# The beginning of a Fourier transform with two feed-forward layers: x on two queues, one contiguous load, w_out's conversion moved, banks copied out earlier

## The chip, the cores and the metric

The kernel runs on one core of a Trainium2 chip. The metric is the time of one execution on the device in microseconds, as the median of three runs. Five engines work side by side, each through its own list of instructions in order: PE multiplies matrices (PEld is its loading of weights), DVE, ACT and POOL work on elements, and SP does nothing but start transfers between memories (DMAs). ACT and POOL can start DMAs too. They wait for each other by semaphores. Products of PE land in banks of the accumulation memory (PSUM), from which DVE or ACT has to copy them before a bank can be used anew.

## The reference

```python
X = np.fft.fft(x, axis=1)                 # x: (2, 3008, 256)
X = np.fft.fft(X, axis=2).real            # -> (6016, 256)
h = X @ w_in                              # w_in (256, 2048)
g = np.where(h > 0.0, h, np.exp(np.minimum(h, 0.0)) - 1.0)     # ELU
X = g @ w_out                             # w_out (2048, 256)
h = X @ w2_in
g = np.maximum(h, 0.0) + alpha * np.minimum(h, 0.0)            # PReLU
out = g @ w2_out
```

The weights are given as float64.

## The kernel before, in words

The transform along the sequence is split in two (3008 = 47 x 64). Stage A (`stage_a`, L143) multiplies x by a 96 x 96 matrix `f47`; x of a batch comes in four pieces c0 to c3 of 96 partitions (`load_x`, L132). The result `uc` is stored to memory as `ud` (`store_u`, L152) and loaded again with other axes on the partitions as `vt` (`load_v`, L164), 1 MB for each block. Stage B (`stage_b`, L195 and L196) multiplies `vt` by `r64` and leaves `zt`, a block of up to 512 columns split in a rounded high part and the rest, `hi` and `lo`. `delta` (L172) makes a correction row from `vt` that goes through memory (`nd`) and comes back as `zb` (`load_zb`, L183). The transform along the 256 columns is folded into the first weights (`w_fold`, L257). There are 2 batches of 3 blocks, and each block's columns come in two halves t = 0 and 1, the frequencies and their mirror images.

Float64 weights are read as pairs of integers and made into float32 on the chip (`conv_y` on ACT, L229; `conv_s`, three operations on DVE, L239 to L243), half a chunk at a time; `w_split` (L282 on ACT, L283 on POOL) makes the hi and lo parts of a chunk of w_out or of the second layer's weights.

Then come 192 ticks, 96 for each layer. A tick t is one block and one slice of 128 of the 2048 hidden columns: `gemm1` (L305) into two PSUM tiles, on DVE `pt` and two `ht` (L386 to L388) in layer 1, the exponential of the ELU on ACT (L403, L404), a tick later the combine on DVE (L419, in layer 2 L421), another tick later `hi` (L395, ACT) and `lo` (L413; POOL in layer 1, DVE in layer 2), and with a lag of three ticks `gemm2` (L319), which adds up in four banks `acc`, one for each output half d and column half t. `SEGS` lists 16 segments of 8 or 16 ticks; at a segment's end, one tick after its last `gemm2`, `evac` copies the four banks out (L350 on DVE for t = 0, L348 on ACT for t = 1). The next segment's first `gemm2` needs them free. The order of everything else is written by hand: `START` lists what happens ahead of tick 0, and tables such as `CONV1`, `CONV2`, `STAGE_A1` and `LOAD_V` hang the rest on ticks, in one of three places of a tick (`pre`, `mid`, `end`). In the function `tick` the order in the program is

```python
        if t - LAG - 1 >= 0 and ticks[t - LAG - 1][2] == ticks[t - LAG - 1][4]:
            evac(*ticks[t - LAG - 1])
        ...
        for fn in end:
            fn()
        if t - LAG in st:
            s = st.pop(t - LAG)
            gemm2(*ticks[t - LAG], s["hi"], s["lo"])
```

Of the kernel before, what the change touches and what calls it, by code (L numbers as in the profile page):

```python
# [7 lines left out]
F32 = mybir.dt.float32  # L8
# [64 lines left out]
def tile_fft_moe_elu_moe_prelu(  # L73
# [296 lines left out]

    def tick(t, pre, mid, end):
# [17 lines left out]
        if t - 2 in st:  # L389
            s = st[t - 2]  # L390
            n = s["n"]
            hi = wk.tile([128, 2, 512], F32R, tag="hi", name="hi")
            lo = wk.tile([128, 2, 512], F32R, tag="lo", name="lo")
            for i in parts(t - 2):
                act(out=hi[:, i, 0:n], in_=s["e"][:, i], func=ACTF.Copy)  # L395
            s["hi"], s["lo"] = hi, lo
# [12 lines left out]
        if t - 2 in st:  # L409
            s = st[t - 2]  # L410
            n = s["n"]
            for i in range(2):
                (nc.gpsimd if s["L"] == 1 else nc.vector).tensor_tensor(out=s["lo"][:, i, 0:n], in0=s["e"][:, i, :],  # L413
                                               in1=s["hi"][:, i, 0:n].bitcast(F32), op=ALU.subtract)
        if t - 1 in st:
            s = st[t - 1]
            if s["L"] == 1:
                for i in parts(t - 1):
                    stt(out=s["e"][:, i], in0=s["e"][:, i], scalar=-1.0, in1=s["h"][:, i], op0=ALU.add, op1=ALU.max)  # L419
            else:  # L420
                stt(out=s["e"], in0=s["e"], scalar=nal_sb[:, s["f"]:s["f"] + 1], in1=s["h"], op0=ALU.mult, op1=ALU.add)  # L421
# [26 lines left out]
    with tc.manual_schedule():  # L448
        nc.sync.dma_start(out=f47_sb, in_=f47)
        for c in range(4):  # L450
            load_x(0, c, 1 if c else 4)
# [150 lines left out]
```

## Time and profile before

| | |
|---|---|
| time before, median of 3 runs | 1028.83 us (1027.87 to 1028.89) |
| profiled execution: its own time / span of its instructions | 1030.7 / 1028.9 us |
| granted clock of PE, mean | 0.985 |
| PE busy | 995.4 us, 97% |
| DVE, ACT, POOL busy | 713.7, 681.8, 353.3 us |

The span is the time from the first to the last instruction; what lies outside it is start and end of the execution. A granted clock of 1.00 is 2.4 GHz, 0.50 is 1.2. The beginning is all that comes ahead of tick 0, the first 45 us. Tick 19 is near 150 us, tick 99 near 511, where layer 2 has just begun.

### The profile page before, as it was taken

To read this page: it belongs to the slowest core of one execution; us is meant where nothing else is said; L and a number is where in the kernel's file an instruction comes from. 1 tells how busy PE (TensorE), PEld (TensorE's weight loads), DVE (VectorE), ACT (ScalarE), POOL (GpSimd) and SP (SyncE) were. 2 spreads that over 40 slices of the span, in tenths; PEclk is the share of its full clock that TensorE was granted. 3 is DMA by queue.
4 is the path that set the end of the run, shared out by engine and by line. 5 is a ranking of instruction groups with operands and counts; after the bars stand their busy time and mean duration, and the time that the engine had idled before them with its cause. 6 is when DMAs were issued, how large, how long until landed. Compare 5 with 4: busy or idle time off the path is not lost.

```text
span 1028.9 us, 11740 instructions
## 1 busy us (share of the span) xinstructions
PE 995.4 (97%) x4348; PEld 805.0 (78%) x4348; DVE 713.7 (69%) x854; ACT 681.8 (66%) x937; POOL 353.3 (34%) x228
## 2 busy tenths in 40 slices
PE   8789999999999999998899999999999999999998
PEld 2467757788888888886678888888888888888887
DVE  1498888978889999999968854654444454455444
ACT  4367866766677777776867765656656666566554
POOL 0157565866688888866611210000000000000000
PEclk9889999999999999999989999999999999999999
DMA  8894422200000000032300000110001001001001
GB/s 246 194 272 134 103 73 49 44 12 1 1 10 1 11 1 1 6 118 88 118 1 1 1 1 1 42 41 1 1 1 39 1 1 42 1 1 41 1 1 39
DMA packets 20513, 44.65 MB, mean 43 GB/s; under 512 B 2116, under 2 KB 9668, under 8 KB 19016
## 3 DMA queue, kind: packets, MB, share of 16 engines
q1 hardware_dynamic: 19152, 42.82, 14.5%
q10 hardware_dynamic: 1176, 1.07, 0.4%
q8 instruction: 34, 0.56, 0.2%
q14 instruction: 23, 0.19, 0.1%
q0 software_dynamic: 128, 0.01, 0.1%
HBM read 31.41 MB, written 12.48 MB: 43 GB/s over the span
## 4 chain that ended last, share of the span: by engine, by line
PE 80%; DVE 13%; DMA 2%; issue 2%; ACT 1%; POOL 0%; SPq 0%; DVEq 0%; ACTq 0%; POOLq 0%
PE acc L319 43%; PE mmt L305 33%; DVE et L419 4%; PE mmt L143 2%; DVE pt L386 2%; DVE ht L388 2%; DVE sg L241 2%; DVE sg L239 1%; DMA vt<-ud 1%; DVE w L243 1%; DMA xc<-x 1%; PE mmt L195 1%; PE mmt L196 1%; DVE ht L387 1%; ACT et L403 1%
## 5 line engine op out<-in xcount | busy, mean ns | idle before, releaser
L319 PE MATMUL acc<-hi,wo 128*128 128x512 f32 (+1 forms) x1536 | 475.1, 391 | 10.6 <-DVE xs L350 8.2
L413 POOL TENSOR_TENSOR lo<-et,hi 128x512 fp32r<-128x512 f32 (+1 forms) x192 | 314.2, 1658 | 94.0 <-ACT hi L395 68.2
L319 PEld LDWEIGHTS acc<-hi,wo 128*128 128x128 f32 x1536 | 291.3, 190 | 69.1 <-ACT wi L282 5.2
L319 PE MATMUL acc<-lo,wo 128*128 128x512 f32 (+1 forms) x768 | 301.8, 393 | 5.4 <-POOL lo L413 5.1
L395 ACT ACTIVATE hi<-et 128x1024 fp32r<-128x1024 f32 (+2 forms) x193 | 199.5, 1034 | 137.1 <-PE acc L319 117.7
L413 DVE TENSOR_TENSOR lo<-et,hi 128x512 fp32r<-128x512 f32 (+1 forms) x192 | 122.1, 678 | 185.1 <-ACT hi L395 184.6
L305 PE MATMUL mmt<-xhi,wi 128*128 128x512 f32 (+1 forms) x768 | 234.9, 387 | 0.0
L319 PEld LDWEIGHTS acc<-lo,wo 128*128 128x128 f32 x768 | 146.3, 190 | 40.0 <-POOL lo L413 11.8
L403 ACT ACTIVATE et<-ht 128x1024 f32<-128x1024 f32 (+2 forms) x97 | 100.5, 1036 | 107.9 <-DVE ht L388 104.1
L305 PEld LDWEIGHTS mmt<-xhi,wi 128*128 128x128 f32 x768 | 144.6, 188 | 28.0
L419 DVE SCALAR_TENSOR_TENSOR et<-et,ht 128x1024 f32<-128x1024 f32 (+2 forms) x97 | 164.1, 1693 | 0.0
L305 PE MATMUL mmt<-zt,wi 128*128 128x512 f32 (+1 forms) x576 | 150.8, 397 | 3.2 <-DVE pt L386 1.3
L407 ACT ACTIVATE ht<-mmt 128x512 f32<-128x512 f32 (+1 forms) x192 | 113.3, 590 | 54.2 <-PE mmt L305 54.1
L305 PE MATMUL mmt<-xlo,wi 128*128 128x512 f32 (+1 forms) x384 | 148.7, 387 | 0.0
L305 PEld LDWEIGHTS mmt<-zt,wi 128*128 128x128 f32 x576 | 108.0, 189 | 30.1 <-issue 3.2
L421 DVE SCALAR_TENSOR_TENSOR et<-et,nal_sb,ht 128x1024 f32<-128x1024 f32 (+1 forms) x96 | 120.8, 1258 | 0.0
L408 ACT ACTIVATE et<-mmt 128x512 f32<-128x512 f32 (+1 forms) x192 | 112.6, 586 | 0.0
L404 ACT ACTIVATE et<-et 128x1024 f32<-128x1024 f32 (+2 forms) x97 | 100.5, 1036 | 3.1
L305 PEld LDWEIGHTS mmt<-xlo,wi 128*128 128x128 f32 x384 | 72.5, 189 | 14.0
L386 DVE SCALAR_TENSOR_TENSOR pt<-zb,an_sb,mmt 128x512 f32<-128x512 f32 (+1 forms) x96 | 70.1, 730 | 15.8 <-PE mmt L305 15.7
L387 DVE TENSOR_TENSOR ht<-pt,mmt 128x512 f32<-128x512 f32 (+1 forms) x96 | 65.1, 678 | 10.4 <-DVE pt L386 0.5
L388 DVE TENSOR_TENSOR ht<-pt,mmt 128x512 f32<-128x512 f32 (+1 forms) x96 | 64.4, 671 | 0.0
(48 smaller groups left out, 426.1 us busy)
## 6 DMA issues: line engine op xcount, KB each, us to landing
w<-w_in SPq DMA_DIRECT2D x8, 1024.0 KB, 17.0
w<-w_out SPq DMA_DIRECT2D x8, 1024.0 KB, 7.6
xc<-x SPq DMA_DIRECT2D x7, 768.0 KB
vt<-ud SPq DMA_DIRECT2D x20, 256.0 KB, 5.3
out_t<-ot SPq DMA_DIRECT2D x16, 256.0 KB, 2.1
ud<-uc SPq DMA_DIRECT2D x4, 768.0 KB, 4.9
ud<-uc SPq DMA_DIRECT2D x8, 256.0 KB, 9.3
out_t<-ot SPq DMA_DIRECT2D x8, 241.0 KB, 2.1
```

Of the source, the lines that this page charges most:

```text
L305: mm(out=p[:, 0:n], lhsT=lhsT, rhs=rhs, start=(i == 0), stop=(i == len(ops) - 1))
L319: mm(out=accs[L, bl][d][t][:, 0:n], lhsT=w[:, a, o, d * 128:(d + 1) * 128], rhs=(hi, lo)[b][:, t, 0:n], start=(f == first and i == 0), sto ...
L386: stt(out=pt[:, 0:n], in0=zb[bl][:, 0:n], scalar=an_sb[:, f:f + 1], in1=p[0], op0=ALU.mult, op1=ALU.add)
L388: tt(out=ht[:, 1, 0:n], in0=pt[:, 0:n], in1=p[1], op=ALU.subtract)
L395: act(out=hi[:, i, 0:n], in_=s["e"][:, i], func=ACTF.Copy)
L403: act(out=s["e"][:, i], in_=s["h"][:, i], func=ACTF.Relu, scale=-1.0)
L404: act(out=s["e"][:, i], in_=s["e"][:, i], func=ACTF.Exp, scale=-1.0)
L407: act(out=s["h"][:, i, :], in_=p[i], func=ACTF.Relu)
L408: act(out=s["e"][:, i, :], in_=p[i], func=ACTF.Relu, scale=-1.0)
L413: (nc.gpsimd if s["L"] == 1 else nc.vector).tensor_tensor(out=s["lo"][:, i, 0:n], in0=s["e"][:, i, :], in1=s["hi"][:, i, 0:n].bitcast(F32) ...
L419: stt(out=s["e"][:, i], in0=s["e"][:, i], scalar=-1.0, in1=s["h"][:, i], op0=ALU.add, op1=ALU.max)
L421: stt(out=s["e"], in0=s["e"], scalar=nal_sb[:, s["f"]:s["f"] + 1], in1=s["h"], op0=ALU.mult, op1=ALU.add)
```

## The change

It has four parts. (1) x of batch 0 is loaded from two queues, partitions 0 to 63 by SP and 64 to 95 by ACT, and c0 in two pieces for each instead of four. (2) `ud` becomes three arrays for each batch, one for each block, laid out so that a block's `vt` is a single contiguous load of 1 MB over 128 partitions; the rows of `r64` are put in the matching order by four loads from POOL's queue. In `START`, block 0's `vt` is asked for after all of stage A, and not in two halves. (3) The first chunk of w_out is loaded ahead of `vt`, its conversion (and the split of its first half) stands ahead of tick 0, three warm-up matmuls stand ahead of `delta`, and tick 0's `gemm2` comes at the end of tick 2 instead of tick 3. (4) At a segment's end `gemm2` and the copies of the t = 0 banks come in the middle of the tick of its last `gemm2`, ahead of that tick's ELU, `lo` and combine, and the t = 1 copies after the combine; before, all four came at the start of the next tick. The table `CONV2` for the second layer's weights is reordered with it.

```diff
 START = [
-    ('load', 'i', 1, 0), ('c256',), ('load', 'i', 1, 1),
-    ('a', 0, 0), ('a', 0, 1), ('a', 1, 0), ('a', 1, 1), ('v', 0, 0, 16), ('r64',), ('a', 2, 0), ('a', 2, 1), ('a', 3, 0),
-    ('conv', 'i', 0, 0), ('a', 3, 1), ('conv', 'i', 0, 1), ('v', 0, 16, 32), ('load', 'o', 1, 0),
-    ('conv', 'i', 1, 0), ('conv', 'i', 1, 1), ('fold', 0), ('an', 0), ('fold', 1), ('delta',), ('zb',),
-    ('u', 32, 64), ('alpha',), ('load', 'o', 1, 1), ('v', 1, 0, 32), ('load', 'x', 1, 0), ('u', 64, 96),
+    ('r64',), ('load', 'i', 1, 0), ('c256',), ('load', 'i', 1, 1), ('load', 'o', 1, 0),
+    ('a', 0, 0), ('a', 0, 1), ('a', 1, 0), ('a', 1, 1), ('a', 2, 0), ('a', 2, 1), ('conv', 'i', 0, 0), ('conv', 'i', 0, 1), ('a', 3, 0),
+    ('a', 3, 1), ('v', 0),
+    ('conv', 'i', 1, 0), ('conv', 'i', 1, 1), ('fold', 0), ('an', 0), ('conv', 'o', 0, 0), ('fold', 1), ('conv', 'o', 0, 1), ('warm',), ('delta',), ('zb',),
+    ('u', 1), ('split', 'o', 0, 0), ('alpha',), ('load', 'o', 1, 1), ('u', 2), ('v', 1), ('load', 'x', 1, 0),
...
 CONV1 = [
-    (('o', 1, 0), (0, 0, 1), (1, 1, 2)),
+    (('o', 1, 0), None, (None, None, 1)),
...
 CONV2 = [
-    (('i', 2, 0), 4, 6, 9, 1, 13, 14),
-    (('o', 2, 0), 7, 12, 15, 1, 18, 18),
-    (('i', 2, 1), 8, 16, 17, 3, 18, 19),
+    (('i', 2, 0), 4, 6, 9, 1, 11, 14),
+    (('i', 2, 1), 8, 15, 16, 3, 17, 18),
+    (('o', 2, 0), 7, 12, 14, 1, 17, 18),
     (('o', 2, 1), 11, 18, 20, 3, 21, 22),
...
-    ud = [dr.tile([32, 96, 256], F32, name=f"ud{b}") for b in range(NB)]
+    ud = [[dr.tile([32, 32, 256], F32, name=f"ud{b}{g}") for g in range(3)] for b in range(NB)]
...
-            nc.sync.dma_start(out=t[:, i * n:(i + 1) * n], in_=x[b, :, c * 8 + i * n:c * 8 + (i + 1) * n, :])
+            for eng, p0, p1 in ((nc.sync, 0, 96),) if b else ((nc.sync, 0, 64), (nc.scalar, 64, 96)):
+                eng.dma_start(out=t[p0:p1, i * n:(i + 1) * n], in_=x[b, p0:p1, c * 8 + i * n:c * 8 + (i + 1) * n, :])
...
-    def load_v(b, g, n0=0, n1=32):
-        if n0 == 0:
-            vt[b, g] = big.tile([128, 8, 256], F32, tag="big", name="vt")
-        for cs in range(2):
-            for h in range(2):
-                m0 = g * 32 + h * 16 + cs * 8
-                p0 = cs * 64 + h * 32
-                nc.sync.dma_start(out=vt[b, g][p0 + n0:p0 + n1],
-                                  in_=ud[b][n0:n1, m0:m0 + 8, :])
+    def load_v(b, g):
+
+        vt[b, g] = big.tile([128, 8, 256], F32, tag="big", name="vt")
+        nc.sync.dma_start(out=vt[b, g], in_=ud[b][g].rearrange("n (q k) j -> (n q) k j", k=8))
+
+    def load_r64():
+        for h in range(2):
+            for cs in range(2):
+                nc.gpsimd.dma_start(out=r64_sb[2 * h + cs::4], in_=r64[cs * 64 + h * 32:cs * 64 + h * 32 + 32, :])
...
     def tick(t, pre, mid, end):
         cur = ticks[t] if t < NT else None
-        if t - LAG - 1 >= 0 and ticks[t - LAG - 1][2] == ticks[t - LAG - 1][4]:
-            evac(*ticks[t - LAG - 1])
...
+        if t == 1:
+            combine(0)
+            split_hi(0)
+            split_lo(0)
+        if t - 2 in st and t > 2:
+            split_hi(t - 2)
         for fn in mid:
             fn()
+        over = t - LAG in st and ticks[t - LAG][2] == ticks[t - LAG][4]
+        if over:
+            s = st.pop(t - LAG)
+            gemm2(*ticks[t - LAG], s["hi"], s["lo"])
+            evac(*ticks[t - LAG], (0,))
...
+        if t - 2 in st and t > 2:
+            split_lo(t - 2)
+        if t - 1 in st and t > 1:
+            combine(t - 1)
+        if over:
+            evac(*ticks[t - LAG], (1,))
         for fn in end:
             fn()
-        if t - LAG in st:
-            s = st.pop(t - LAG)
-            gemm2(*ticks[t - LAG], s["hi"], s["lo"])
+        u = {2: 0, 3: None}.get(t, t - LAG)
+        if u in st:
+            s = st.pop(u)
+            gemm2(*ticks[u], s["hi"], s["lo"])
...
-            load_x(0, c, 1 if c else 4)
+            load_x(0, c, 1 if c else 2)
```

`combine`, `split_hi` and `split_lo` hold the lines for the combine, `hi` and `lo` that stood in `tick` before, and `evac` takes the halves t that it is to copy.

The first place is SP's list of transfers at the beginning, before (f_sb is `f47`, c_sb `c256`, r_sb `r64`):

```order
L132 DMA xc<-x 96x512 x4
L132 DMA xc<-x 96x2048 x3
L216 DMA w_105<-w_in 128x2x1024
L475 DMA c_sb<-c 128x2x256
L216 DMA w_108<-w_in 128x2x1024
L164 DMA vt<-ud_81 16x2048 x4
L476 DMA r_sb<-r 128x320
L164 DMA vt<-ud_81 16x2048 x4
L216 DMA w_187<-w_out 128x4x512
L183 DMA zb<-nd_83 128x512
```

and in the change:

```order
L133 DMA xc<-x 64x1024 x2
L133 DMA xc<-x 64x2048 x3
L219 DMA w_116<-w_in 128x2x1024
L495 DMA c_sb<-c 128x2x256
L219 DMA w_119<-w_in 128x2x1024
L219 DMA w_121<-w_out 128x4x512
L163 DMA vt<-ud_81 128x2048
L186 DMA zb<-nd_87 128x512
```

w_out's first chunk has moved ahead of `vt`, which is one load in place of eight, and the other 32 partitions of x have gone to ACT's list.

The second place is DVE's list from the first weights to tick 1, before (w_187 is the float64 chunk 0 of w_out, w_307 what it is converted to):

```order
L263 TENSOR_TENSOR wi_216<-mmt,wi_216 128x512 x2
L200 TENSOR_TENSOR zt<-mmt,zt 128x2x256 x2
L386 SCALAR_TENSOR_TENSOR pt<-zb,an_sb,mmt 128x512
L387 TENSOR_TENSOR ht<-pt,mmt 128x512
L388 TENSOR_TENSOR ht<-pt,mmt 128x512
L239 TENSOR_SCALAR sg<-w_187 128x512
L241 SCALAR_TENSOR_TENSOR sg<-w_187,sg 128x512
L243 SCALAR_TENSOR_TENSOR w_307<-w_307,sg 128x512
L386 SCALAR_TENSOR_TENSOR pt<-zb,an_sb,mmt 128x512
```

and in the change (w_121 is that chunk now):

```order
L266 TENSOR_TENSOR wi_225<-mmt,wi_225 128x512 x2
L242 TENSOR_SCALAR sg<-w_121 128x512
L244 SCALAR_TENSOR_TENSOR sg<-w_121,sg 128x512
L246 SCALAR_TENSOR_TENSOR w_219<-w_219,sg 128x512
L203 TENSOR_TENSOR zt<-mmt,zt 128x2x256 x2
L409 SCALAR_TENSOR_TENSOR pt<-zb,an_sb,mmt 128x512
L410 TENSOR_TENSOR ht<-pt,mmt 128x512
L411 TENSOR_TENSOR ht<-pt,mmt 128x512
L409 SCALAR_TENSOR_TENSOR pt<-zb,an_sb,mmt 128x512
```

The conversion has moved from between the ticks to ahead of `zt`.

The third place is DVE's list at the end of layer 1's last segment (ticks 98 and 99), before (w_3777 is chunk 1 of the second w_out):

```order
L413 TENSOR_TENSOR lo<-et,hi 128x512 x2
L421 SCALAR_TENSOR_TENSOR et<-et,nal_sb,ht 128x1024
L239 TENSOR_SCALAR sg<-w_3777 128x512
L241 SCALAR_TENSOR_TENSOR sg<-w_3777,sg 128x512
L243 SCALAR_TENSOR_TENSOR w_4084<-w_4084,sg 128x512
L350 COPY xs<-acc_3503 128x482
L350 COPY xs<-acc_3505 128x482
```

and in the change:

```order
L353 COPY xs<-acc_3503 128x482
L353 COPY xs<-acc_3505 128x482
L393 TENSOR_TENSOR lo<-et,hi 128x512 x2
L380 SCALAR_TENSOR_TENSOR et<-et,nal_sb,ht 128x1024
L242 TENSOR_SCALAR sg<-w_3777 128x512
L244 SCALAR_TENSOR_TENSOR sg<-w_3777,sg 128x512
L246 SCALAR_TENSOR_TENSOR w_4090<-w_4090,sg 128x512
```

The two copies have moved from behind `lo`, the combine and the conversion to ahead of them.

## Rows read from the trace of the kernel before

**Rows 1.** The page: busy time by engine; then groups: busy us, mean ns, idle.

```profile
PE 995.4 (97%) x4348; PEld 805.0 (78%) x4348; DVE 713.7 (69%) x854; ACT 681.8 (66%) x937; POOL 353.3 (34%) x228
...
L413 POOL TENSOR_TENSOR lo<-et,hi 128x512 fp32r<-128x512 f32 (+1 forms) x192 | 314.2, 1658 | 94.0 <-ACT hi L395 68.2
...
L395 ACT ACTIVATE hi<-et 128x1024 fp32r<-128x1024 f32 (+2 forms) x193 | 199.5, 1034 | 137.1 <-PE acc L319 117.7
```

**Rows 2.** Timeline of PE: start us, us, what, count, [idle before <-releaser].

```profile
12.05 12.21 PE L143 MATMUL mmt<-xc,f_sb 96*96 96x512 f32 x24 [2.77 <-DMA xc<-x]
...
37.29 0.37 PE L172 MATMUL mmt<-r_sb,vt 128*8 128x64 f32 x2 [4.01 <-DMA vt<-ud]
...
45.45 4.76 PE L305 MATMUL mmt<-zt,wi 128*128 128x512 f32 x18 [1.18 <-ACT zt L199]
...
56.38 1.63 PE L319 MATMUL acc<-hi,wo 128*128 128x512 f32 x2 [2.35 <-ACT hi L395]
...
155.38 0.71 PE L319 MATMUL acc<-hi,wo 128*128 128x512 f32 x2 [3.34 <-DVE xs L350]
...
515.63 1.19 PE L319 MATMUL acc<-hi,wo 128*128 128x512 f32 x2 [4.84 <-DVE xs L350]
```

**Rows 3.** Stretches: us, busy of PE, PEld, DVE, ACT, POOL, granted clock, DMA, GB/s.

```profile
12.05:16.04 3.99, 3.98 (x6) 1.45 (x7) 0.00 (x0) 1.18 (x2) 0.00 (x0) 0.57 0.98 231
...
37.81:43.35 5.54, 5.54 (x27) 5.54 (x27) 0.00 (x0) 0.21 (x1) 0.17 (x1) 0.50 0.52 161
58.45:63.83 5.38, 5.38 (x13) 4.22 (x14) 5.28 (x6) 5.32 (x7) 5.24 (x3) 0.50 1.02 346
...
67.59:71.68 4.09, 4.09 (x37) 3.98 (x38) 3.95 (x7) 1.53 (x2) 1.51 (x1) 1.00 1.00 287
155.99:159.40 3.41, 3.41 (x10) 2.67 (x9) 3.27 (x4) 1.99 (x3) 2.39 (x2) 0.50 0.01 2
515.63:521.20 5.57, 5.57 (x13) 4.41 (x14) 4.10 (x5) 0.46 (x1) 1.15 (x1) 0.50 0.01 3
```

**Rows 4.** The chain that ended last, first 90 us: start us, us, what.

```profile
3.06 8.86 DMA xc<-x
...
30.72 6.37 DMA vt<-ud
...
38.16 2.37 DMA nd<-dt
...
73.38 2.75 PE acc L319 x12
```

**Rows 5.** DMA views: 6:14, 16:23, 52:58, 430:520 us; zb and nd to landing.

```profile
DMA packets 270, 1.94 MB, mean 243 GB/s; under 512 B 32, under 2 KB 32, under 8 KB 33
...
DMA packets 1339, 2.68 MB, mean 382 GB/s; under 512 B 76, under 2 KB 893, under 8 KB 1336
...
DMA packets 222, 1.26 MB, mean 211 GB/s; under 512 B 64, under 2 KB 64, under 8 KB 69
...
w<-w_in SPq DMA_DIRECT2D x4, 1024.0 KB, 5.4
...
DMA to landing us min/median/max: 3.2/4.9/6.6
```

**Rows 6.** Timeline: the last store of uc (ACT) and the loads of vt (SP).

```profile
24.92 0.31 ACTq L152 DMA_DIRECT2D ud<-uc  x1
...
28.04 3.11 SPq L164 DMA_DIRECT2D vt<-ud  x4
```

**Rows 7.** Timeline of DVE: tick 0's pt, and the conversion behind its ht.

```profile
46.83 0.75 DVE L386 SCALAR_TENSOR_TENSOR pt<-zb,an_sb,mmt 128x512 f32<-128x512 f32 x1 [0.60 <-PE mmt L305]
...
48.88 0.42 DVE L239 TENSOR_SCALAR sg<-w 128x512 int32<-128x512 int32 x1
```

**Rows 8.** Timeline of DVE: the combine ahead of the copies at tick 19.

```profile
152.62 2.01 DVE L419 SCALAR_TENSOR_TENSOR et<-et,ht 128x1024 f32<-128x1024 f32 x1
```

**Rows 9.** Timeline of DVE: the conversion ahead of the copies at tick 99.

```profile
510.06 1.51 DVE L239 TENSOR_SCALAR sg<-w 128x512 int32<-128x512 int32 x1
```

More of the change, by code (lines that the diff above doesn't have):

```diff
@@ L146, in stage_a, with store_u @@
         if i == 1 and b == 1:
-            store_u(b, c, 0, 96)
+            for g in range(3):
+                store_u(b, c, g)
         if i == 1 and b == 0:
-            store_u(b, c, 0, 32, nc.scalar)
-    def store_u(b, c, m0, m1, eng=nc.sync):
-        eng.dma_start(out=ud[b][c * 8:(c + 1) * 8, m0:m1, :].rearrange("n m j -> m n j"), in_=uc[b, c][m0:m1])
+            store_u(b, c, 0, nc.scalar)
+    def store_u(b, c, g, eng=nc.sync):
+        eng.dma_start(out=ud[b][g][c * 8:(c + 1) * 8].rearrange("n m j -> m n j"),
+                      in_=uc[b, c][g * 32:(g + 1) * 32])
     vt = {}
-    def load_v(b, g, n0=0, n1=32):
-        if n0 == 0:
-            vt[b, g] = big.tile([128, 8, 256], F32, tag="big", name="vt")
-        for cs in range(2):
-            for h in range(2):
-                m0 = g * 32 + h * 16 + cs * 8
-                p0 = cs * 64 + h * 32
-                nc.sync.dma_start(out=vt[b, g][p0 + n0:p0 + n1],
-                                  in_=ud[b][n0:n1, m0:m0 + 8, :])
+    def load_v(b, g):
[5 more added lines that the diff above has]
+                nc.gpsimd.dma_start(out=r64_sb[2 * h + cs::4], in_=r64[cs * 64 + h * 32:cs * 64 + h * 32 + 32, :])
     def delta(b, gs):
@@ L322, in tile_fft_moe_elu_moe_prelu, with evac @@
     ys = {}
-    def evac(L, bl, f, first, last):
+    def evac(L, bl, f, first, last, ts):
         n = BLK_N[bl % 3]
-        ac = accs.pop((L, bl))
+        ac = accs[L, bl]
         done = last == NFT - 1
-        if first == 0 and (L == 1 or not done):
+        if first == 0 and (L == 1 or not done) and ts[0] == 0:
             if L == 1:
@@ L334, in evac @@
                 ys[bl] = wp.tile([128, 2, 2, 512], F32, tag="sc", name="ys")
-        for t in range(2):
+        for t in ts:
             for d in range(2):
@@ L369, in parts, with combine, split_hi, split_lo @@
         return (slice(0, 1), slice(1, 2)) if t == 0 else (slice(0, 2),)
+    def combine(t):
+        s = st[t]
+        if s["L"] == 1:
+            for i in parts(t):
+                stt(out=s["e"][:, i], in0=s["e"][:, i], scalar=-1.0, in1=s["h"][:, i], op0=ALU.add, op1=ALU.max)
+        else:
+            stt(out=s["e"], in0=s["e"], scalar=nal_sb[:, s["f"]:s["f"] + 1], in1=s["h"], op0=ALU.mult, op1=ALU.add)
+    def split_hi(t):
+        s = st[t]
+        s["hi"] = wk.tile([128, 2, 512], F32R, tag="hi", name="hi")
+        s["lo"] = wk.tile([128, 2, 512], F32R, tag="lo", name="lo")
+        for i in parts(t):
+            act(out=s["hi"][:, i, 0:s["n"]], in_=s["e"][:, i], func=ACTF.Copy)
+    def split_lo(t):
+        s = st[t]
+        n = s["n"]
+        for i in range(2):
+            (nc.gpsimd if s["L"] == 1 else nc.vector).tensor_tensor(
+                out=s["lo"][:, i, 0:n], in0=s["e"][:, i, :], in1=s["hi"][:, i, 0:n].bitcast(F32), op=ALU.subtract)
     def tick(t, pre, mid, end):
         cur = ticks[t] if t < NT else None
-        if t - LAG - 1 >= 0 and ticks[t - LAG - 1][2] == ticks[t - LAG - 1][4]:
-            evac(*ticks[t - LAG - 1])
         for fn in pre:
@@ L388, in tick @@
                 tt(out=ht[:, 1, 0:n], in0=pt[:, 0:n], in1=p[1], op=ALU.subtract)
[L389 to L396, printed above, removed]
+        if t == 1:
[4 more added lines that the diff above has]
+            split_hi(t - 2)
         for fn in mid:
             fn()
+        over = t - LAG in st and ticks[t - LAG][2] == ticks[t - LAG][4]
[3 more added lines that the diff above has]
+            evac(*ticks[t - LAG], (0,))
         if cur:
@@ L408, in tick @@
                     act(out=s["e"][:, i, :], in_=p[i], func=ACTF.Relu, scale=-1.0)
[L409 to L421, printed above, removed]
+        if t - 2 in st and t > 2:
[4 more added lines that the diff above has]
+            evac(*ticks[t - LAG], (1,))
         for fn in end:
             fn()
-        if t - LAG in st:
-            s = st.pop(t - LAG)
-            gemm2(*ticks[t - LAG], s["hi"], s["lo"])
+        u = {2: 0, 3: None}.get(t, t - LAG)
+        if u in st:
+            s = st.pop(u)
+            gemm2(*ticks[u], s["hi"], s["lo"])
     hooks = {"pre": {}, "mid": {}, "end": {}}
@@ L469, in tile_fft_moe_elu_moe_prelu @@
             "b": lambda: stage_b(0, 0),
-            "u": lambda m0, m1: [store_u(0, c, m0, m1) for c in range(4)],
-            "v": lambda g, n0, n1: load_v(0, g, n0, n1),
+            "u": lambda g: [store_u(0, c, g) for c in range(4)],
+            "v": lambda g: load_v(0, g),
             "alpha": lambda: nc.sync.dma_start(out=al_sb, in_=alpha),
@@ L475, in tile_fft_moe_elu_moe_prelu @@
             "c256": lambda: nc.sync.dma_start(out=c256_sb, in_=c256.rearrange("(k p) f -> p k f", p=128)),
-            "r64": lambda: nc.sync.dma_start(out=r64_sb, in_=r64),
+            "r64": load_r64,
             "warm": warm_up,
@@ L482, in tile_fft_moe_elu_moe_prelu @@
             for i, ts in enumerate(halves):
-                at_conv(ts[0], [ts[1]] * 3, *key, i)
+                if ts and ts[0] is not None:
+                    at_conv(ts[0], [ts[1]] * 3, *key, i)
             for i, ts in enumerate(halves):
-                if key[0] == "o":
+                if key[0] == "o" and ts:
                     at_split(ts[2], *key, i)
@@ L516, in tile_fft_moe_elu_moe_prelu @@
                 at(t, split_x, bl, i // 2, i % 2, where="mid")
-        for t in range(NT + LAG + 1):
+        for t in range(NT + LAG):
             tick(t, *(hooks[w].get(t, []) for w in ("pre", "mid", "end")))
```

## Prediction

> **What bounds the kernel now.** I read the page's busy shares first: PE is busy 995.4 us of a span of 1028.9 [rows 1], so the whole kernel is matmuls and a change can win only PE's idle time and the time that PE runs slowly. The timeline of PE then shows where the idle time is: six waits of over 1 us make up 18.5 us of it [rows 2]. Four stand ahead of 57 us: for the second piece of x (2.77), for block 0's vt (4.01), for zt (1.18) and for the first tick's hi (2.35). Two stand at segment ends, at ticks 19 and 99, where the second gemm waits for banks that DVE has not copied out: 3.34 and 4.84. The table of stretches adds the clock: behind each of these the granted clock falls to 0.50, which is 1.2 of 2.4 GHz [rows 3]; in the four stretches at 0.50 and the one at 0.57 PE is busy 23.9 us, of which about 11.7 would go at full clock. So 18.5 + 11.7 = 30 us is about all that the places touched by this change can give back.
>
> **Arrival of x.** x for batch 0 is 3.15 MB. In 6 to 14 us one queue moved it at 243 GB/s [rows 5]. What two queues move of it no row shows. Lower bound: 211 GB/s, the stretch 52 to 58 us, whose loads and stores cover 96 or 32 partitions as the new ones cover 64 and 32. Upper bound: 382 GB/s, the stretch 16 to 23 us in which SP's and ACT's queues both ran. The rows are nearly equally far, so I take 300. From about 2.6 us on that is 10.5 us, the end at 13.1, and c1 is there after two thirds of it, at 9.6 and not 11.92 [rows 4]. PE's first 8 records end at 9.28 (12.05 less the wait). 24 records took 12.21 us, of which (1 - 0.57) x 3.99 = 1.7 is slow clock [rows 2, 3]: 3.5 us for 8. Stage A ends at 9.6 + 10.5 = 20.1, not at 24.26.
>
> The Trainium skill, *DMA: Bandwidth & Descriptors*, section "Rules for kernel authors", speaks against this edit: loads of disjoint partition groups and loads spread over SP and ACT run on the same 16 engines and gain nothing but issue time. By that rule x would keep its 243 GB/s; the row of 382 does not refute it, since other tiles moved there. It is rival 1 below.
>
> **vt in one contiguous load.** Before, the last store of uc was issued at 24.92 and the load that waits for it at 28.04, 3.1 later; vt landed at 37.09, 9.05 after that [rows 4, 6]. In the change ACT converts w_in c0 ahead of the last chunk's four copies, which PE's products pace until 20.1; the store goes out at about 20.9 and vt is issued at 24.0. The w_out load now stands ahead of vt on SP's queue: 4.4 MB of weights, c256 and stores at 382 GB/s take 11.7 us from 13.1 to 24.8, so moving w_out past vt costs 0.8 here. The nearest rows for a load of 1 MB are 5.4 us, alone, and 9.05, that of before in eight pieces; the contiguous one is nearest to the first: 24.8 + 5.4 = 30.2, or 33.9.
>
> PE has work until then: two folds, 16 records, 7.0 us to 27.1, some 0.5 of waits on DVE and ACT, and three warm-up matmuls, 6 records or 2.6 us: 30.2 also. Those matmuls are new work but stand where PE waited 4.01. Stage B starts at 30.2 in place of 37.29: **-7.1**. PE is not idle ahead of it, so I expect the full clock: the same stage for block 1 took 4.09 at 1.00, while this one took 45.45 - 1.18 - 37.29 = 6.98, nearly all at 0.50 [rows 2, 3]: **-2.9**. The first gemm starts at about 35.5 and not 45.45. zb needs delta, whose store began 0.87 after stage B did (38.16 - 37.29), the store of nd (2.37) and its own issue and load (0.4 and 3.2) [rows 2, 4, 5], together 6.9 after 30.2: 37.1, where DVE's pt would come at 46.83 - 10.0 = 36.8 [rows 7]. That leaves -9.7 for both. Bounds: at 382 GB/s PE paces stage A, -10.5; at 211 GB/s with vt at 9.05 the start of stage B stays where it is and only the clock is won, -3. The four r64 loads on POOL's queue and the x issues on ACT's cost nothing: both engines have no other work then. Without that cover r64 would delay delta, by one issue each.
>
> **Ticks 0 to 4.** Before, the conversion of w_out c0 sits between the ticks on DVE, from 48.88 on [rows 7], and a second time a tick later. Now it is done ahead of zt, where DVE waits for vt. The first hi follows pt by about 5.6 us (pt and two ht 48.88 - 46.83 = 2.05, the same again, half of a combine 1.0 [rows 8], half of a hi 0.5 [rows 1]) and not by 56.38 - 46.83 = 9.55, and the second gemm of tick 0 comes a tick earlier. From pt to the second gemm of tick 2 before: 73.38 - 46.83 = 26.55 [rows 4, 7]. With lo on POOL next in the chain (1.66 each [rows 1]) I count 21.5 at full clock, -5. But PE still idles over 3 us here, as it did ahead of the 0.50 of 58 to 64 us; if the slow stretch stays, it eats nearly all: 0. I take **-3**.
>
> **Banks ahead of the ELU.** At tick 19 DVE ran a combine of 2.01 ahead of the two copies [rows 8]; now the copies go first, and DVE's banks are free 2.0 us sooner. But ACT's two copies stay behind its ELU, and the delayed combine makes the next tick's lo late: I let these two take back 1.4, so that 0.6 is won, and with it the slow stretch behind, 1.7 [rows 3]: **-2.3**, bounds 0 and -5.0 (all of 3.34 and 1.7).
>
> At tick 99 the copies stood behind a combine and a conversion of three operations that began at 510.06, and PE's wait for them ended at 515.63 [rows 2, 9]. Now they stand ahead of both, and the reordered table moves one w_in conversion a tick forward; so the 4.84 and the 2.8 of slow clock, 7.6, could go. Late next: the same conversion now runs ahead of lo for tick 97, and the one moved forward ahead of the last ELU combine of layer 1. What these take back lies between nothing and all but about 1; I take 2.6, about half of the time from 510.06 to 515.63 that the conversion and the copies took together: **-5**, bounds -1 and -7.6. Elsewhere the other 13 evacuations wait for nothing in the trace of before, so I put no gain there.
>
> **Sum**: -9.7 - 3 - 2.3 - 5 = -20. The profiled execution took 1030.7, 1.8 outside its span, and the runs' median is 1028.8; the span goes to 1008.9 and the median to **1008.8**. Own range of this case 1003 to 1014.
>
> **Rivals.**
> 1. Two queues bring x no sooner than one, at 243 GB/s [rows 5]. Stage A ends at 24.3, the last store goes out at 24.9, vt at 28.0 + 5.4 = 33.4; folds and warm-up end about 35. Stage B -2.3, its clock -2.9: -5 in place of -9.7, 1013.5. For it: the 211 GB/s row, where few partitions are covered. This is the outcome by the rule of the Trainium skill's page above.
> 2. The banks' waits only move. DVE has no pause ahead of 510, and work is only moved in its queue; lo then waits where the copies did. -1 in place of -7.3: 1015. For it: from the conversion's first operation to the end of PE's wait went 5.6 us [rows 2, 9], so a conversion ahead of lo is dear.
> 3. The slow clock stays in the start: if PE pauses between fold and delta as before, stage B keeps its 6.98 and ticks 0 to 4 their 26.55: 1015.
> 4. Slower. In each of 15 segment ends DVE now stands in its queue before a bank that the second gemm is still filling, with combine and lo behind it. If each cost PE p, the sum is -20 + 7.3 + 15p; from p = 1.0 on the kernel is slower, at 2.0 it is 1046. Against it: the second gemm takes 2.75 us [rows 4], its first half is done when DVE's two ht are, and a combine has about two ticks until PE needs its lo.
> 5. No measurable change: the start comes out at its lower bound and the ends at theirs, -3 - 0 - 1 and a little new wait: 1026 to 1029.
>
> **Chances.** Forecast 0.57, rival 1 0.15, rival 2 0.12, rival 3 0.08, rival 4 0.03, rival 5 0.05. All but the last two are faster by over 0.2% (2.1 us, about what a measurement of this kernel can tell from none); half of rival 5 is too: faster 0.94, same 0.03, slower 0.03. The range reaches down to all bounds but the clock's, 1001, and up past the rivals 1 to 3, to 1018.
>
> **What would show it.** Right: the wait for c1 under 1 us; stage B at 29 to 32 us at a clock of 1.00; the first pt near 37; no wait of over 2.5 us on the copied banks at ticks 19 and 99, and no stretch at 0.50 behind tick 99. Wrong step by step: x still near 243 GB/s until 15 us; vt over 7 us from issue to landing; folds or w_out's conversion ending later than vt; the slow stretch still 10 us long at ticks 0 to 4; lo in place of the banks as PE's wait at tick 100. A first pt later than 42 us, or new waits at the ends that had none, would make the forecast wrong.

## The result, and the profile after

The changed kernel takes 1013.5 us (median of four runs, 1012.98 to 1013.99), the kernel before in the same job 1028.38 (1027.87 to 1028.89): a ratio of 0.9855, 95% interval 0.9838 to 0.9872. That is 14.9 us faster, where 20 were forecast. The profiled execution took 1012.98, so from profile to profile the gain is 17.7: that of before lay 2.3 above its median.

The page after, which answers to [rows 1]: busy time by engine, and the group of lo.

```profile
PE 986.8 (98%) x4354; PEld 797.8 (79%) x4354; DVE 711.0 (70%) x854; ACT 680.1 (67%) x937; POOL 350.7 (35%) x232
...
L393 POOL TENSOR_TENSOR lo<-et,hi 128x512 fp32r<-128x512 f32 (+1 forms) x192 | 306.5, 1618 | 108.3 <-ACT hi L387 65.3
```

PE has six more matmul records (the warm-up, 2.74 us of work) and is yet busy 8.6 us less; no work was taken from it, so what went is slow clock. Its idle time, the span of 1011.2 less the busy time, went from 33.5 to 24.4.

The timeline of PE after, for [rows 2]: start us, us, what, count, wait before it and what ended it.

```profile
7.89 3.76 PE L144 MATMUL mmt<-xc,f_sb 96*96 96x512 f32 x8 [2.10 <-DMA xc<-x]
13.44 10.51 PE L144 MATMUL mmt<-xc,f_sb 96*96 96x512 f32 x24 [1.78 <-DMA xc<-x]
...
34.28 0.28 PE L175 MATMUL mmt<-r_sb,vt 128*8 128x64 f32 x2
...
39.62 4.80 PE L308 MATMUL mmt<-zt,wi 128*128 128x512 f32 x18 [1.18 <-ACT zt L202]
...
46.49 0.73 PE L322 MATMUL acc<-hi,wo 128*128 128x512 f32 x2 [2.08 <-ACT hi L387]
...
143.65 0.70 PE L322 MATMUL acc<-hi,wo 128*128 128x512 f32 x2 [1.39 <-DVE xs L353]
...
501.45 0.72 PE L322 MATMUL acc<-hi,wo 128*128 128x512 f32 x2 [0.57 <-ACT xs L351]
```

Two rows went the wrong way: PE waits for the first piece of x too, until 7.89, and c1 is there at 13.44 and not at 12.05. Stage B no longer waits, but starts at 34.28 where 30.2 was forecast. Tick 19's wait fell from 3.34 to 1.39, tick 99's from 4.84 to 0.57.

The stretches after, for [rows 3]; columns as there, with the granted clock third from the right.

```profile
13.44:23.95 10.51, 10.51 (x25) 4.15 (x26) 2.79 (x5) 7.15 (x13) 0.00 (x0) 1.00 1.01 333
34.28:38.44 4.16, 4.16 (x37) 3.86 (x36) 1.31 (x2) 0.84 (x2) 2.00 (x2) 1.00 0.29 65
46.49:51.73 5.24, 4.61 (x13) 3.42 (x14) 3.06 (x4) 5.18 (x7) 4.33 (x3) 0.67 1.04 347
143.65:149.00 5.35, 4.95 (x20) 3.57 (x20) 5.25 (x7) 4.98 (x7) 2.61 (x3) 1.00 0.06 2
501.45:507.00 5.55, 5.47 (x22) 4.04 (x23) 3.94 (x6) 4.86 (x9) 2.85 (x2) 1.00 0.02 3
```

Stage A, stage B and both segment ends run at 1.00. One slow stretch is left ahead of 500 us, behind PE's wait of 2.08 for the first hi.

The chain that ended last, after, for [rows 4].

```profile
10.04 15.00 DMA w<-w_in
...
28.93 2.84 PE mmt L260 x6
31.77 2.58 PE mmt L480 x6
...
40.99 0.76 DVE pt L409
...
63.57 2.73 PE acc L322 x12
```

The chain enters stage B through w_in's second chunk, its conversion, the last fold and the warm-up, not through vt: the two arrive together. The last row is tick 2's second gemm; before it started at 73.38 [rows 4], 9.8 later. So at the first pt (46.83 before, 40.99 now) the lead is 5.8, at tick 2 it is 9.8. Pairing the second gemms by their order, it stays at 9.8 up to tick 14 (ends at 142.69 and 132.88), is 11.2 behind tick 19 (180.84 and 169.60), 11.7 at tick 88 (472.70 and 460.97) but 11.3 again ahead of tick 99 (508.06 and 496.80), and 17.6 behind tick 99 (564.77 and 547.19). These four steps, 5.8, 4.0, about 1.5 and 6.3, are the gain between these two profiles.

The DMA of 6 to 14 us after, for the first of [rows 5], by queue (q1 is SP's, q10 ACT's, q0 POOL's), and the stretch 11 to 16, in which nearly all that moves is on SP's queue, where the 64-partition part of x stands.

```profile
DMA packets 417, 2.00 MB, mean 250 GB/s; under 512 B 127, under 2 KB 127, under 8 KB 207
...
q1 hardware_dynamic: 246, 1.42, 76.0%
q10 hardware_dynamic: 97, 0.49, 23.9%
q0 software_dynamic: 74, 0.08, 4.5%
...
11.00:16.00 5.00, 3.22 (x8) 1.06 (x7) 0.00 (x0) 2.21 (x4) 0.00 (x0) 1.00 1.01 206
```

Two queues moved 250 GB/s where one had moved 243, and not 300. Of these 2.00 MB, 0.08 are r64's on POOL's queue; SP's and ACT's queues together moved 1.91, or 239 GB/s.

The last store of uc and the load of vt, for [rows 6], and the page's row of all six loads of vt, with the median from issue to landing:

```profile
24.74 0.31 ACTq L154 DMA_DIRECT2D ud<-uc  x1
...
29.16 0.35 SPq L163 DMA_DIRECT2D vt<-ud  x1
...
vt<-ud SPq DMA_DIRECT2D x6, 1024.0 KB, 4.8
```

### The profile page after: what moved, and what is told of

Same layout as the page of the kernel before. It is cut to its first block, busy times and chain, and to the rows that moved or that the text cites. A ratio compares the mean times of both kernels' runs of the same rounds, so it can differ in the third digit from the quotient of the medians.

```text
span 1011.2 us, 11723 instructions
## 1 busy us (share of the span) xinstructions
PE 986.8 (98%) x4354; PEld 797.8 (79%) x4354; DVE 711.0 (70%) x854; ACT 680.1 (67%) x937; POOL 350.7 (35%) x232
## 4 chain that ended last, share of the span: by engine, by line
PE 79%; DVE 12%; issue 3%; DMA 3%; ACT 2%; POOL 1%; SPq 0%; DVEq 0%; ACTq 0%; POOLq 0%
PE acc L322 43%; PE mmt L308 33%; DVE et L378 4%; DVE ht L411 2%; DVE pt L409 2%; DMA w<-w_in 1%; DVE sg L244 1%; DVE sg L242 1%; PE mmt L260 1%; PE mmt L144 1%; DMA xc<-x 1%; DVE w L246 1%; PE mmt L198 1%; DVE ht L410 1%; PE mmt L199 1%
## 5 line engine op out<-in xcount | busy, mean ns | idle before, releaser
L393 POOL TENSOR_TENSOR lo<-et,hi 128x512 fp32r<-128x512 f32 (+1 forms) x192 | 306.5, 1618 | 108.3 <-ACT hi L387 65.3
L322 PEld LDWEIGHTS acc<-lo,wo 128*128 128x128 f32 x768 | 145.1, 189 | 40.4 <-POOL lo L393 12.1
L378 DVE SCALAR_TENSOR_TENSOR et<-et,ht 128x1024 f32<-128x1024 f32 (+2 forms) x97 | 166.4, 1716 | 0.7 <-ACT et L430 0.7
## 6 DMA issues: line engine op xcount, KB each, us to landing
w<-w_out SPq DMA_DIRECT2D x8, 1024.0 KB, 11.3
```

Of the source, the lines that this page charges most:

```text
L322: mm(out=accs[L, bl][d][t][:, 0:n], lhsT=w[:, a, o, d * 128:(d + 1) * 128], rhs=(hi, lo)[b][:, t, 0:n], start=(f == first and i == 0), sto ...
```

## The experiments

Twelve kernels ran, one of them the kernel before again. That kernel's median was 1026.6 to 1028.4 in the five jobs, a spread of 1.8, so a difference of 1 to 2 us between kernels of different jobs is at the edge of what the times can tell.

**x on one queue again**

```diff
-            for eng, p0, p1 in ((nc.sync, 0, 96),) if b else ((nc.sync, 0, 64), (nc.scalar, 64, 96)):
+            for eng, p0, p1 in ((nc.sync, 0, 96),):
...
-            load_x(0, c, 1 if c else 2)
+            load_x(0, c, 1 if c else 4)
```

> The changed kernel with x for batch 0 on SP's queue alone again, the first chunk in four parts as before; all other parts of the change stay. Theory (two queues bring x no sooner, and the share of the smaller part comes early while the larger part's first pieces come late): the first matmul of stage A starts near 5.6 us and not 7.89, the wait for the second chunk ends near 11.9 and not 13.44, stage A ends near 22.4 and not 23.95, vt lands 0 to 1.5 us sooner, and the time stays within 1.5 us of the changed kernel's 1013.5: 1012 to 1014. Rival (two queues did help, as forecast, only less): x lands later than in the changed kernel, stage A ends at 25 or later, and the time is 1015 to 1018.

1013.79 (1012.56 to 1015.76; ratio 0.9862, 0.9842 to 0.9881). Its timeline of PE, and its DMA from 6 to 14 us:

```profile
5.48 2.74 PE L144 MATMUL mmt<-xc,f_sb 96*96 96x512 f32 x6
...
12.07 12.21 PE L144 MATMUL mmt<-xc,f_sb 96*96 96x512 f32 x24 [2.23 <-DMA xc<-x]
...
DMA packets 317, 1.92 MB, mean 241 GB/s; under 512 B 54, under 2 KB 54, under 8 KB 93
```

The first matmuls are 2.4 sooner and c1 1.4 sooner, as the theory said; its stage A then ran into a slow stretch (12.21 us for the 24 records that took 10.51 in the changed kernel) and ended at 24.28, not at 22.4, so the trace, which is that of the slowest of the five runs, does not show what an undisturbed start would give. The time is the same: the second queue gained nothing.

**The old ends on the new beginning, and the new ends on the old beginning**

```diff
 def tick(t, pre, mid, end):
+        if t - LAG - 1 >= 0 and ticks[t - LAG - 1][2] == ticks[t - LAG - 1][4]:
+            evac(*ticks[t - LAG - 1], (0, 1))
...
-        over = t - LAG in st and ticks[t - LAG][2] == ticks[t - LAG][4]
-        if over:
...
```

The first kernel is the changed one with these lines and layer 2's old conversion table; the second is the kernel before with the change's `over` branch and its new table.

> The changed kernel with the four copies of a segment's banks at the start of the next tick again, the second gemm at the end of its tick, and the conversion table of layer 2 as before: the beginning of the change alone. Theory (the ends gave 1.5 at tick 19 and 6.3 at tick 99, the beginning the rest): the waits of 3.3 at tick 19 and 4.8 at tick 99 are back with their slow clock, +7 to +8: 1020 to 1022. Rival (the ends' waits belong to the phase that the beginning sets, and would have gone with the new beginning alone): +0 to +3, 1013 to 1016.

> The kernel before with the new places of the bank copies and the new conversion table alone, its beginning as it was. Theory (the two halves of the change add up): 7 to 8 below before, 1020 to 1022, and together with the run of the new beginning alone the two gains sum to the whole of 15. Rival (the gain at the ends needs the new beginning): 0 to 3 below before, 1025 to 1028; or the other way, most of the 15 comes from the ends, below 1017.

The first took 1018.89 (1017.67 to 1022.29), 5.4 above the changed kernel, with a ratio of 0.9917 (0.9896 to 0.9938); the second 1019.79 (1016.70 to 1022.97), 8.5 below before, ratio 0.9926 (0.9901 to 0.9950). PE's waits at the ends, the first kernel's:

```profile
147.10 0.70 PE L322 MATMUL acc<-hi,wo 128*128 128x512 f32 x2 [3.33 <-DVE xs L353]
...
507.60 0.77 PE L322 MATMUL acc<-hi,wo 128*128 128x512 f32 x1 [4.67 <-DVE xs L353]
```

and the second's:

```profile
148.88 0.70 PE L319 MATMUL acc<-hi,wo 128*128 128x512 f32 x2 [1.43 <-DVE xs L350]
...
506.91 0.73 PE L319 MATMUL acc<-hi,wo 128*128 128x512 f32 x2 [0.68 <-ACT xs L348]
```

The waits follow the code of the ends whatever the beginning is: the rival falls, though the first kernel lost less than the 7 to 8 expected. The beginning alone is worth about 9.4 and the ends alone 8.5; added to the other, the beginning is worth 6.3 and the ends 5.4. The two alone make 17.9, 3 more than the whole of 14.9. These two kernels' runs spread over 5 to 6 us, too wide to tell whether the gains overlap.

**The kernel before once more**

> The kernel before once more, unchanged, as a control. Theory (its profiled execution of 1030.7 lay 2 us above its median of 1028.4 because a stretch of slow clock was longer in it): another profile is 1 to 2 us shorter, and the difference stands in a stretch at a clock of 0.50, in the start or behind tick 99. Rival (profiling itself costs it 2 us): the profile shows 1030 to 1031 again.

1025.32, in a job in which eleven runs of it lay between 1023.57 and 1030.42. Its stage A went at 1.00, where [rows 3] has 0.57 for the first 4 us:

```profile
10.77:23.00 12.23, 11.26 (x26) 4.09 (x26) 2.58 (x5) 8.27 (x14) 0.00 (x0) 1.00 1.02 320
34.98:40.76 5.78, 5.78 (x36) 5.48 (x36) 0.00 (x0) 0.21 (x1) 0.75 (x1) 0.70 0.66 183
```

and stage B took 5.78 and not 6.98; c1 was there at 10.77 and not at 12.05, and tick 2 is 3.5 earlier than in the first profile. So where the clock is low in the beginning, and when c1 comes, differ from run to run, by more than the 1 to 2 us expected: a profile of before is good to about 3 us here, and of the 17.7 between the two profiles 2 to 3 are that. This bears on the steps above. Against this second profile (first pt at 43.31) they are 2.3, 4.0, 0.7 and 5.1, 12.1 together. The 4.0 of ticks 0 to 4 holds with both; the start's share is 2.3 or 5.8 and that of tick 99 5.1 or 6.3, by which of the two is taken.

**x padded to 128 partitions, on one queue**

```diff
-            t = big.tile([96, 8, 256], F32, tag="big", name="xc")
+            t = big.tile([128, 8, 256], F32, tag="big", name="xc")
...
+            for eng, p0, p1 in ((nc.sync, 0, 128),):
...
-    f47_sb = const.tile([96, 96], F32, name="f47_sb")
+    f47_sb = const.tile([128, 96], F32, name="f47_sb")
```

> The changed kernel with x for batch 0 padded to 128 partitions (32 rows of zeros, and the DFT matrix f47 with 32 rows of zeros), on SP's queue alone in whole 1 MB loads, the first of them in two halves; the output is the same, 4.2 MB move and not 3.15. Theory (what held x back is the rate of loads that cover 96, 64 or 32 partitions, 211 to 275 GB/s, where loads of 128 partitions moved at 382): the 4.2 MB are in by 13 to 14 us and not 17 to 18, stage A ends near 20 to 21 and not 23.95, the first pt comes 3 us sooner, and the time is 1009 to 1011. Rival (the rate belongs to the first microseconds of a program or to the source, whatever the partitions): a third more bytes at 265 GB/s, x later by 3 us, and the time 1015 to 1018.

1009.44 (1009.24 to 1010.00; ratio 0.9821, 0.9803 to 0.9839), 4 us below the changed kernel, with a third more bytes of x. Its DMA from 6 to 14 us, and its timeline of PE:

```profile
DMA packets 561, 3.37 MB, mean 421 GB/s; under 512 B 97, under 2 KB 97, under 8 KB 189
...
5.58 14.77 PE L144 MATMUL mmt<-xc,f_sb 128*96 128x512 f32 x32
...
30.75 0.28 PE L175 MATMUL mmt<-r_sb,vt 128*8 128x64 f32 x2
```

421 GB/s against 241 on the same queue: the rate hung on the partitions that a load covers. PE goes through stage A without a wait, to 20.35. Every lead from tick 2 on is 3.5 above the changed kernel's. The edit pads x of batch 1 as well, whose loads come later; as the 3.5 does not change from tick 2 to behind tick 99, they gave nothing. The theory holds.

**The same x split over two queues, in halves and in whole loads**

```diff
-            for eng, p0, p1 in ((nc.sync, 0, 128),):
+            for eng, p0, p1 in ((nc.sync, 0, 128),) if b else ((nc.sync, 0, 64), (nc.scalar, 64, 128)):
```

```diff
+            for eng, p0, p1 in (((nc.scalar if b == 0 and (c + i) % 2 else nc.sync), 0, 128),):
```

> The kernel with x padded to 128 partitions, each chunk of batch 0 split into rows 0 to 63 on SP's queue and rows 64 to 127 on ACT's. Theory (a load that covers few partitions moves slowly, whatever else runs beside it): near 265 to 300 GB/s, the 4.2 MB are in 3 us or more later than by 14.5, stage A ends 2 to 4 us later, 1012 to 1014. Rival (what counts is that the loads under way together cover 128 partitions, on however many queues): over 380 GB/s, within 0.7 us of 1009.44.

> The kernel with x padded to 128 partitions, the loads of batch 0 whole (all 128 rows) and given in turn to SP's and to ACT's queue. Theory (what took 7.5 us when each chunk was split into rows 0 to 63 and 64 to 127 is the form of those loads, not the second queue): over 380 GB/s again, 1009 to 1011, at most 1 us above 1009.44 because neighbouring chunks now share the rate and the earlier one lands later. Rival (two queues at once disturb one another, whatever they move): near 250 GB/s and 1014 to 1017.

In halves 1016.97 (1016.07 to 1017.75), 7.5 worse than one queue; in whole loads 1013.29 (1012.64 to 1014.46), 3.9 worse. Their DMA from 6 to 14 us, the halves first, then PE's start with the whole loads and the load that it waited for (from the chain that ended last):

```profile
DMA packets 386, 1.96 MB, mean 245 GB/s; under 512 B 94, under 2 KB 94, under 8 KB 186
...
DMA packets 644, 3.36 MB, mean 420 GB/s; under 512 B 126, under 2 KB 126, under 8 KB 323
...
8.66 15.42 PE L144 MATMUL mmt<-xc,f_sb 128*96 128x512 f32 x32 [2.88 <-DMA xc<-x]
...
1.20 7.33 DMA xc<-x
```

Both halves under way together are still slow, so it is the form of each load. Whole loads keep the rate whatever the queue; there both theories missed the time, because the two queues are served side by side (in these 8 us SP's moved 1.64 MB and ACT's 1.58). So c0's first part, issued on SP's queue at 1.20, shared the rate with the loads on ACT's, and PE waited for it until 8.66, where it had x at 5.58 with one queue. Stage A, which took 15.42 us of PE from there, ended at 24.08, as in the changed kernel.

**vt in pieces, no warm-up, the old table**

```diff
-        nc.sync.dma_start(out=vt[b, g], in_=ud[b][g].rearrange("n (q k) j -> (n q) k j", k=8))
+        for cs in range(2):
+            for h in range(2):
+                ...
+                nc.sync.dma_start(out=vt[b, g][p0:p0 + 32], in_=ud[b][:, m0:m0 + 8, :])
```

> The changed kernel with block 0 of vt no longer contiguous: one scratch tensor again and the load of 1 MB in four of 32 partitions each, r64 in one load. Theory (the contiguous load is the part of the beginning that gave most): vt takes 7 to 9 us from issue to landing and not 5.1, stage B starts 2 to 4 us later than 34.28, and PE waits for vt, which brings back the slow clock in stage B: +4 to +6, 1017 to 1020. Rival (the gain came from issuing all of vt at once behind one wait, not from its layout): vt lands within 1 us of the changed kernel's, the time within 1 us of 1013.5.

1015.47 (1014.76 to 1016.44), +2.0: between the two. The last piece was issued at 30.2 and took 5.5 to land, so vt was there at 35.7; the contiguous one is issued at 29.2 and takes 4.8, 34.0. But PE too came late in that profile (its stage A ended at 25.24, 1.3 later), and stage B's wait ended on DVE. So contiguity is worth at most 2 here; how much of the 2 is its own stays open. The edit takes contiguity from all six loads of vt, but the lead is 2.4 smaller at tick 2 and still 2.4 behind tick 99, so only block 0's counts.

```diff
-    ('conv', 'i', 1, 0), ..., ('conv', 'o', 0, 1), ('warm',), ('delta',), ('zb',),
+    ('conv', 'i', 1, 0), ..., ('conv', 'o', 0, 1), ('delta',), ('zb',),
```

> The changed kernel without the three warm-up matmuls between the folds and delta; nothing of the result depends on them. Theory (they only fill PE's wait for vt, which lands at 34.3 with or without them): stage B starts at 34.3 as before, PE pauses 2.6 us ahead of it and stage B runs at a clock of 0.50, 6.9 us and not 4.1: +2 to +3, 1015.5 to 1016.5. Rival (a pause of 2.6 us does not cost the clock, or the slow stretch only moves up from the first hi to here): within 1 us of 1013.5.

1015.27 (1012.11 to 1018.35), +1.8. Its timeline of PE at stage B, and that stretch:

```profile
34.37 0.36 PE L175 MATMUL mmt<-r_sb,vt 128*8 128x64 f32 x2 [2.36 <-DMA vt<-ud]
...
34.37:40.11 5.74, 5.74 (x36) 5.34 (x36) 1.43 (x3) 0.84 (x2) 1.99 (x2) 0.70 0.43 109
```

Stage B starts where it did and takes 5.74 at 0.70, not 4.16 at 1.00: the warm-up cost nothing, because vt lands no sooner, and bought 1.6 us of clock here. The trace bears the theory out; the time, just under its range, does not settle it, as the five runs spread over 6.2 us.

```diff
-    (('i', 2, 0), 4, 6, 9, 1, 11, 14),
-    (('i', 2, 1), 8, 15, 16, 3, 17, 18),
-    (('o', 2, 0), 7, 12, 14, 1, 17, 18),
+    (('i', 2, 0), 4, 6, 9, 1, 13, 14),
+    (('o', 2, 0), 7, 12, 15, 1, 18, 18),
+    (('i', 2, 1), 8, 16, 17, 3, 18, 19),
```

> The changed kernel with the copies ahead of the ELU but layer 2's conversion table of before. Theory (at tick 99 the copies' new place gives most, the table little): +0 to +1.5, 1013.5 to 1015, with a wait under 2 us at tick 99. Rival (the conversions that stood at ticks 18 and 19 behind the segment's end made the wait): the wait near tick 99 is back at 3 us or more with a slow stretch behind it, +4 to +6: 1017 to 1020.

1015.50 (1014.66 to 1016.54), +2.0, just over the theory's bound. At tick 99 PE waits for a weight split of POOL and not for banks:

```profile
501.52 0.50 PE L322 MATMUL acc<-hi,wo 128*128 128x512 f32 x1 [1.28 <-POOL wo L286]
```

Its lead shrinks by 1.1 there and by 0.9 in the start, which the table does not touch. The place of the copies gives the most of tick 99, the table about 1.

**w_out converted between the ticks again**

```diff
-        if t == 1:
-            combine(0)
-            split_hi(0)
-            split_lo(0)
...
-    (('o', 1, 0), None, (None, None, 1)),
+    (('o', 1, 0), (0, 0, 1), (1, 1, 2)),
...
-        u = {2: 0, 3: None}.get(t, t - LAG)
+        u = t - LAG
```

> The changed kernel with the first w_out chunk back where it was: loaded behind vt, converted and split at ticks 0 and 1, the first combine and hi at their usual ticks, the second gemm of tick 0 at tick 3. Theory (the earlier conversion gave the 4 us that the profiles show between the first pt and tick 4): vt is issued 1 us sooner, but the first hi stands about 9.5 us behind the first pt and not 5.5, and the whole is +2.5 to +4: 1016 to 1017.5. Rival (the second gemm only had to be done later: PE takes the first gemms of the next ticks meanwhile, and what it won was the clock): +0 to +1.5, 1013.5 to 1015.

1016.52 (1016.00 to 1016.67), +3.0, as the theory said. Its PE waits in tick 0 to 3:

```profile
45.90 0.97 PE L308 MATMUL mmt<-zt,wi 128*128 128x512 f32 x3 [1.30 <-DVE pt L409]
47.28 1.48 PE L308 MATMUL mmt<-zt,wi 128*128 128x512 f32 x3 [0.42 <-DVE ht L411]
50.73 1.63 PE L322 MATMUL acc<-hi,wo 128*128 128x512 f32 x2 [1.97 <-ACT hi L387]
```

Here vt is issued 2.8 after the last store, in the changed kernel 4.4 after it (29.16 less 24.74): w_out's load ahead of it costs 1.6. (In the kernel with vt in pieces that load stands ahead too, but the store goes out 1.3 later, at 26.02, and vt is issued 2.9 after it, so the order alone does not make the cost.) It moves nothing, since stage B starts at 34.48 here behind folds and warm-up.

**PE's wait for the first hi filled**

```diff
+        if t == 2:
+            accs[1, 0] = [[pa.tile(...) for k in range(2)] for d in range(2)]
+            for i in range(3):
+                mm(out=accs[1, 0][0][0][:, 0:320], lhsT=r64_sb[:, 0:128], rhs=r64_sb, start=True, stop=True)
```

> The kernel with x padded to 128 partitions, and three dummy matmuls of 320 columns on PE between the first gemm of tick 2 and the second gemm of tick 0, where PE waits 2.1 us for the first hi; they write a bank that the second gemm then starts over. Theory (the one stretch of 3.4 us at a clock of 0.50 left in the beginning comes from that wait): the wait falls under 0.7 us of idle, the stretch goes, and the time falls by 1.5 to 1.8 from 1009.44: 1007.6 to 1008. Rival (the slow stretch comes from what PE did earlier, or only moves to the next wait): 1009 to 1010, and a stretch at 0.50 still stands ahead of 60 us.

1010.01 (1009.81 to 1010.21), 0.6 above the kernel without it, which the times of two jobs cannot tell from no difference: the stretch went as the theory said, the gain did not come. Its timeline of PE:

```profile
43.05 0.73 PE L322 MATMUL acc<-hi,wo 128*128 128x512 f32 x2 [0.50 <-ACT hi L387]
...
50.56 0.50 PE L322 MATMUL acc<-lo,wo 128*128 128x512 f32 x1 [0.42 <-POOL lo L393]
...
52.79 0.51 PE L322 MATMUL acc<-lo,wo 128*128 128x512 f32 x1 [0.57 <-POOL lo L393]
...
59.87 0.50 PE L308 MATMUL mmt<-zt,wi 128*128 128x512 f32 x1 [0.98 <-ACT dt L178]
```

The slow stretch is gone, and tick 0's second gemm ends 1.5 sooner. Then PE waits for lo twice and for dt, and by tick 2 it is 0.8 behind: POOL and ACT pace these ticks, and the slow clock had cost nothing there. Why it ends behind, and not level, is not shown.

## Why the prediction was off by a quarter

**Arrival of x failed.** "I take 300": the two queues moved 250, and the 64-partition part alone 206. The upper bound of 382 was mostly from loads of 128 partitions; the experiments show that it was their form, not the second queue, that made it. The lower bound's loads covered 96 and 32 partitions, like those asked about, and were not "nearly equally far". Stage A ended at 23.95 and not 20.1, stage B started at 34.28 and not 30.2, and the start gave 5.8 and not 9.7 (2.3 against the second profile of before). The rate is not all of it: at 250 the forecast's own reckoning, c1 after two thirds of x, gives 11.0, and c1 was there at 13.44; what held it up the rest is not shown. The r64 loads, put at nothing because POOL has no other work then, took 0.08 of the 2.00 MB that moved from 6 to 14 us. This is rival 1, whose price of 1013.5 was met; that it was met to the decimal is luck, as its terms of 5, 3, 2.3 and 5 were 5.8, 4.0, 1.5 and 6.3 in one pair of profiles and 2.3, 4.0, 0.7 and 5.1 in the other. With x at 421 GB/s, more than the 300 reckoned with, the forecast's own numbers come out: stage A ends at 20.35 (20.1 forecast), stage B starts at 30.75 (30.2), the time is 1009.44 (1008.8).

The rule of the Trainium skill, *DMA: Bandwidth & Descriptors*, section "Rules for kernel authors", that was set against this edit holds: 96 partitions split over two queues gained nothing (1013.5 against 1013.79), and 128 so split lost 7.5 us. *SBUF — State Buffer*, section "Door 1: The DMA port swizzle", says that partitions 0 to 63 reach only 8 of the 16 ports through which DMA writes, half the rate. The trace agrees: 206 GB/s against 421. It does not say why two halves under way at once reached 245 and no more, or 96 partitions 241; that stays open.

**vt and stage B.** The load took 4.8 for the 5.4 assumed. It was issued 4.4 after the last store, for 3.1 and 0.8 forecast; w_out's part was 1.6 and not 0.8. As forecast, folds and warm-up end when vt lands, so neither alone would move stage B. Its clock gave 2.8 of the 2.9 (1.6 against the second profile of before); rival 3 falls. The first pt follows stage B's start by 6.7 (6.9).

**Ticks 0 to 4.** 3 forecast, 4.0 in the profiles, 3.0 in the times. The slow stretch of which I feared that it "eats nearly all" stands on time that POOL and ACT set.

**Segment ends.** Tick 19: 2.3 forecast, about 1.5 found (0.7 against the second profile); ACT's copies behind its ELU are late next, as said, with 0.40. Tick 99: 5 forecast, 6.3 found (5.1 against the second profile). PE does not wait there for lo, through which, with a late combine, 2.6 was to be taken back; the one wait left is 0.57, for ACT's copies. The two together are 7.8 in the profiles for 7.3 (5.8 against the second profile), 5.4 to 8.5 in the times. Rival 2 falls, and rival 4 too: the longest wait of PE behind tick 19 is 1.1, for lo, and before had one of 1.2 there.

**The list of waits was not whole.** The trace of before has four more waits of PE over 1 us: 2.01 ahead of its first matmul, 1.08 in the folds, 1.32 for pt at 51.54 and 1.19 for lo at 183.83. And the clock did not fall behind each wait: behind that for zt it was 1.00. The sum rests on neither.

## What to carry to other kernels

Before reckoning with a second queue, look at how many partitions each load covers: here padding 96 rows to 128 beat every split that was tried, although it moved a third more bytes. When a row is to price an unseen transfer, take the one of the same form, not the mean of two. And a slow or idle stretch need not be worth its time: filled ahead of stage B it gave 1.6 us, filled ahead of the first hi nothing, because other engines set the pace there. Fill it and see who waits next.

## What was unexpected of the hardware

On one queue, loads of 96 partitions moved at 241 GB/s and of 128 at 421; two halves of 64 at once on two queues at 245, no better than one of 96. Two queues are served side by side, so that a small load on the second delays the first pieces on the first: PE's first wait ended at 7.89 with the split and it had x at 5.48 without. The times of one kernel spread very unevenly: 6.9 us over eleven runs of before in one job and 1.0 over four in another, 1.0 over four of the change, 6.2 over five without the warm-up, 0.8 over five with x padded. Whether fewer waits in the start bring them closer together is not shown.
